# Attention, capped routing, experts and a gated block on one core: conversion in 512 columns, a rewritten compaction, and changed ends of the attention

## The chip, the cores and the metric

The kernel runs on one core of a Trainium2 chip. The metric is the device time of that core in microseconds (us); smaller is better. Five engines run side by side, each with its own queue that it works through in order: PE (matmul), DVE (vector), ACT (scalar), POOL (GpSimd) and SP, which here only issues DMAs. An instruction that waits holds everything behind it in its queue.

## The reference

```
scores = scale * matmul(q_c, [mem_k, k_ctx].T)        # chunk 32, left 16, right 8, 8 memory keys
a = exp(scores - max); a = a / (sum(a) + 1e-9); out_c = matmul(a, [mem_v, v_ctx])
x = out as [3072 tokens, 512]
logits = x @ w_gate                                   # 8 experts
for idx in argsort(-logits.flatten()):                # greedy; 384 tokens for each expert
    token, e = idx // 8, idx % 8
    if token not assigned and count[e] < 384: assign
x[mask_e] = relu(x[mask_e] @ w1[e]) @ w2[e]           # 512 -> 1024 -> 512
h = x @ w_in                                          # 512 -> 1024
solu = h * softmax(h)
ln = (solu - mean) / sqrt(var + 1e-6) * g_ln
return ln @ w_out                                     # 1024 -> 512
```

Everything is float32 at the inputs except `w_in` and `w_out`, which come as float64 (64-bit words) and have to be converted on the chip.

## The kernel before, in words

**Attention** takes 24 tiles of 128 tokens (`NT`). For tile `i` the loop emits parts of five tiles: the sums of tile i-1, the scores of tile i (`s`, PE), their maximum `mx` and the subtraction `p` (DVE), the exponential (ACT, `p<-p`), then the product with `v`, the transposes `xtp`, and the gate's matmuls. SP loads `qt`, `kd` and `vd` of each tile; `kd` and `vd` are rings of 5 and 4 buffers, of which only parts are loaded, so all nine are set to zero at the start. The gate works on four tiles at a time (`gate`, 32 columns of PE for each tile), except in the last four tiles, which `gate_last` takes one by one. Then all logits stand in `L`.

**Routing** goes through 8 rounds; one expert is filled in each. A round takes the maximum `m` of `L`, runs two searches of four steps (`ge` on DVE, `r<-oh,ge` on PE, `sat` on DVE, `second` on PE, `base` on DVE), and then `compact` makes the list `idx` of the 384 tokens of the expert. With it POOL gathers the rows `xg` from DRAM, and `iw` picks the expert's weights.

**Experts** then run on PE, all matmuls as sums of three products of a high and a low part (`xh`, `xl`, `w1h`, `w1l` and so on): `g12` (`h<-xh,w1h` to `y<-hh,w2h`), `g3` (`h<-in_h,yh`) and `g4` (`o<-out_h,lh`). The order is g12(0), g3(0), g12(1), g3(1), g4(0), g12(2), and so on. In the order of emission the routing of round r+1 lies beside round r.

**Conversion** (class `Fixed`) makes `in_h`, `in_l`, `out_h`, `out_l` from the 64-bit `w_in` and `w_out`, in chunks of 256 columns, 16 for each matrix: a DMA `raw`, ACT `v<-raw`, DVE `e<-raw`, `v<-v,e`, `e<-v`, `e<-raw,e`, then ACT `in_h` or `out_h`, and POOL `v<-v,in_h` and `in_l<-v,e` (for `w_out`: POOL `v<-v,e`, ACT `out_h`, DVE or POOL `out_l`). `raw`, `v` and `e` are rings of three.

**What sets the order.** A planner (`Pace`) keeps a modelled clock for each engine. "Beside" jobs (conversion, routing) are generators; when the main stream calls `tick()`, it lets those go on whose next step fits by the model (`limit` bounds the rank of jobs that may run, `late` and `DUE_OUT` push the conversion of `w_out`). The result is a fixed order for each engine; the chip waits only for semaphores. Nearly every instruction is recorded by one helper, line 398 before and 420 after, so rows are told apart by tile names.

Of the kernel before, what the change touches and what calls it, by code (L numbers as in the profile page):

```python
# [48 lines left out]
DUE_OUT = 5.42  # L49
# [11 lines left out]
def attention(nc, tc, q, kx, vx, wgx, ident, x_dram, L, consts, beside):  # L61

    with ExitStack() as ctx:
# [34 lines left out]
        consts()  # L98

# [79 lines left out]
        def gate(u, js=range(4)):  # L179
            if js[0] == 0:  # L180
                G[u] = ps.tile([128, 128], F32, tag="t", name="g")
# [16 lines left out]
        def gate_t(u):  # L198
            g = ps.tile([128, 4, 32], F32, tag="t", name="g")
            nc.tensor.transpose(g, G.pop(u), ident)  # L200
            nc.vector.tensor_scalar(L[:, 4 * u:4 * u + 4, :], g[:, :, 0:E], 0.0, None, op0=ALU.add)

        for i in range(NT + 5):
            n = 0
# [26 lines left out]
            if i > NT:  # L231
                gate_last(i - 5)
# [5 lines left out]
class Pace:  # L238
# [61 lines left out]
    def cost(self, eng, op, outs, ins, kw):  # L300
# [9 lines left out]
        t = (0.108 if op == "transpose" else 0.06 * n / 128 if kw.get("tile_position") else  # L310
# [99 lines left out]
class Fixed:  # L410
# [6 lines left out]
    CHUNK = 256  # L417
# [24 lines left out]
    def chunk(self, m, n, lead=0.0):  # L442
# [6 lines left out]
        if wide:  # L449
            yield from self.take("raw", 3)  # L450
            while self.hold:
                yield 0.0
            r = self.tmp.tile([128, C, 2], I32, tag="raw", name="raw", bufs=3)
# [4 lines left out]
            yield from self.take("v", 3)  # L458
            v = self.tmp.tile([128, C], F32, tag="v", name="v", bufs=3)
            e = self.tmp.tile([128, C], F32, tag="e", name="e", bufs=3)  # L460
            vi, ei, top = v.bitcast(I32), e.bitcast(I32), r[:, :, 1]
            nc.scalar.activation(v, top.bitcast(F32), AF.Copy, scale=2.0 ** -112)
            yield "spare", "dve"
            V.tensor_scalar(ei, top, -0x80000000, None, op0=ALU.bitwise_and)
            yield "act"
# [7 lines left out]
        else:  # L473
            yield from self.take("v", 3)
            v = self.tmp.tile([128, C], F32, tag="v", name="v", bufs=3)
# [44 lines left out]
class Route:  # L520
# [6 lines left out]
    def __init__(self, ctx, nc, tc, L, beside):  # L527
# [4 lines left out]
        self.held, self.stage = False, 0  # L532

    def consts(self):
# [9 lines left out]
        self.tri = k.tile([128, 128], F16, name="tri")  # L544
        V.tensor_scalar(self.tri, self.row, col, None, op0=ALU.is_gt)
# [18 lines left out]
        iota(self.cp[:, :, 0], [[1, NT]], 0, 0)
        V.tensor_copy(self.cp[:, :, 1], col.to_broadcast([128, NT]))
# [99 lines left out]
    def rounds(self):  # L665
# [3 lines left out]
        for r in range(E):  # L669
# [6 lines left out]
            if r + 1 < E:  # L676
# [12 lines left out]
                yield from self.search(lo, oh, zero, r, r + .5)  # L689
                th = self.found  # L690
# [71 lines left out]
    def compact(self, r, s1, sl):  # L762

        nc = self.nc
        V, T = nc.vector, nc.tensor
        low = self.t("low", [NT], I32)
        V.tensor_scalar(low, sl, 127, None, op0=ALU.bitwise_and)
        b = self.t("b", [NT, TT])
        V.tensor_scalar(b[:, :, 2], sl, 256.0, None, op0=ALU.is_ge)
        V.tensor_scalar(b[:, :, 0], sl, 128.0, None, op0=ALU.is_lt)  # L770
        yield "spare", "dve"
        cc = self.t("cc", [2 * TT])
        rhs = self.t("rhs", [NT, 2, TT], BF)
        half, part = NT // 2, NT // 4
        for c0 in (0, half):
            ohl = []
            for c1 in (c0, c0 + part):
                o = self.w.tile([128, part, 128], BF, tag="ohl", name="ohl", bufs=2)
                V.tensor_tensor(o, self.row[:, None, :].to_broadcast([128, part, 128]),
                                low[:, c1:c1 + part, None].to_broadcast([128, part, 128]), op=ALU.is_equal)  # L780
                ohl.append(o)
                if c1 == 0:
                    V.scalar_tensor_tensor(b[:, :, 1], b[:, :, 0], -1.0, b[:, :, 2], op0=ALU.mult, op1=ALU.subtract)
                    V.tensor_scalar(b[:, :, 1], b[:, :, 1], 1.0, None, op0=ALU.add)
                    V.tensor_tensor(b, b, s1[:, :, None].to_broadcast([128, NT, TT]), op=ALU.mult)
                    for a in range(2):
                        V.tensor_tensor(rhs[:, :, a], b, self.cp[:, :, a:a + 1].to_broadcast([128, NT, TT]),
                                        op=ALU.mult)
                yield 0.0
            yield "dve"  # L790
            p = yield from self.take()
            for c in range(half):
                T.matmul(p[:, 0:2 * TT], ohl[c // part][:, c % part],
                         rhs[:, c0 + c].rearrange("p a t -> p (a t)"), start=c == 0, stop=c == half - 1)
            yield "pe"
            if c0 == 0:
                V.tensor_copy(cc, p[:, 0:2 * TT])
            else:
                V.tensor_tensor(cc, cc, p[:, 0:2 * TT], op=ALU.add)
            self.held = False  # L800
        idx = self.k.tile([128, TT], I32, name=f"idx{r}")
        V.scalar_tensor_tensor(idx, cc[:, 0:TT], 128.0, cc[:, TT:2 * TT], op0=ALU.mult, op1=ALU.add)
# [3 lines left out]
class Experts:  # L806
# [159 lines left out]
    def g3(self, r, t, between):  # L966
# [3 lines left out]
        for half in range(2):  # L970
            n = 0
            s = slice(half * 512, half * 512 + 512)
            for dt in range(4):
                self.need("y", r, dt)
                self.fixed.need(0, self.beside, {4 * dt + 2 * half, 4 * dt + 2 * half + 1})
# [273 lines left out]
```

## Time and profile before

| | before |
|---|---|
| median of 3 runs | 793.64 us (793.4 to 796.08) |
| the profiled execution | 792.05 us, span 790.3 us |
| mean granted clock | 0.953 |
| busy PE / DVE / ACT / POOL | 717.0 / 550.4 / 340.9 / 207.4 us |
| chain that ended last | PE 69%, DVE 19%, issue 4%, POOL 3%, ACT 2%, DMA 2% |

In the forty slices of the page PE is at 9 tenths nearly throughout, except in the first six slices (attention, 7 to 9), in slices 7 and 8 (3 and 6; the first routing round) and in slice 15 (4). In that one slice outside the first 160 us PE's clock falls as well. The chain that ended last runs on DVE to about 140 us and on PE after it.

### The profile page before, as it was taken

How to read it: one execution, taken by the hardware profiler on the slowest of the kernel's cores; microseconds unless marked ns; L12 is line 12 of the kernel's file. 1: busy time of each engine (PE TensorE's matmuls, PEld its weight loads, DVE VectorE, ACT ScalarE, POOL GpSimd, SP SyncE). 2: the span in 40 equal slices, each digit the busy share in tenths (PEclk: the TensorE clock that was granted, in tenths of full speed). 3: DMA queues.
4: the chain of work that ended last, by engine and by line, in shares of the span. 5: the costliest groups of instructions: out<-in, count | busy, mean ns of one | idle time of the engine just before them, and what ended most of it. 6: DMA issues, size and time to landing. Idle time of an engine off the chain costs nothing.

```text
span 790.3 us, 14784 instructions
## 1 busy us (share of the span) xinstructions
PE 717.0 (91%) x5728; PEld 619.6 (78%) x5728; DVE 550.4 (70%) x1536; ACT 340.9 (43%) x680; POOL 207.4 (26%) x288
## 2 busy tenths in 40 slices
PE   6988963699999949999999999999999999999993
PEld 5766653688789737998899889888988898899883
DVE  7787967699999974993798389838973952563150
ACT  1566630243574443431653174227324642463170
POOL 4344520631621342003300520052014211400121
PEclk7999995699999978999999999999999999999997
DMA  7999891720620340102600340053006110600100
GB/s 248 336 331 337 292 349 56 231 85 29 219 87 27 100 141 30 64 1 81 213 0 1 128 165 1 1 177 118 1 14 210 70 41 27 209 19 0 41 15 27
DMA packets 32326, 89.37 MB, mean 113 GB/s; under 512 B 4480, under 2 KB 4608, under 8 KB 32256
## 3 DMA queue, kind: packets, MB, share of 16 engines
q0 software_dynamic: 13056, 46.14, 17.2%
q1 hardware_dynamic: 19200, 42.29, 15.6%
q8 instruction: 45, 0.74, 0.4%
q14 instruction: 25, 0.20, 0.1%
HBM read 75.83 MB, written 12.58 MB: 112 GB/s over the span
## 4 chain that ended last, share of the span: by engine, by line
PE 69%; DVE 19%; issue 4%; POOL 3%; ACT 2%; DMA 2%; POOLq 0%; DVEq 0%
PE h L398 30%; PE y L398 17%; PE o L398 15%; DVE e L398 4%; PE tp L398 4%; PE r L398 3%; DVE sum L398 2%; DVE p L398 2%; DVE mx L398 2%; DVE v L398 1%; DMA xg<-x_dram,idx 1%; ACT p L398 1%; DVE ge L398 1%; DVE nm L398 1%; DMA raw<-in_win_dram 1%
## 5 line engine op out<-in xcount | busy, mean ns | idle before, releaser
L398 PE MATMUL y<-hh,w2h 128*128 128x384 f32 x256 | 91.7, 358 | 5.4 <-DVE e L398 5.4
L398 POOL DMA_INDIRECT out_dram<-ob,idx x24 | 26.1, 1089 | 265.6 <-ACT ob L398 223.4
L398 PE MATMUL y<-hl,w2h 128*128 128x384 f32 x256 | 88.9, 347 | 0.1
L398 PE MATMUL o<-out_h,lh 128*128 128x512 f32 x192 | 78.4, 409 | 11.2 <-ACT out_h L398 11.2
L398 PE MATMUL y<-hh,w2l 128*128 128x384 f32 x256 | 87.4, 341 | 0.0
L398 POOL DMA_INDIRECT raw<-in_w_dram,iw x64 | 62.6, 978 | 73.4 <-DVE w1l L398 27.9
L398 PE MATMUL o<-out_l,lh 128*128 128x512 f32 x192 | 76.6, 399 | 1.2 <-DVE out_l L398 1.2
L398 PE MATMUL h<-in_h,yh 128*128 128x512 f32 x192 | 76.7, 399 | 0.0
L398 PE MATMUL h<-in_l,yh 128*128 128x512 f32 x192 | 76.4, 398 | 0.0
L398 PE MATMUL o<-out_h,ll 128*128 128x512 f32 x192 | 76.4, 398 | 0.0
L398 DVE TENSOR_REDUCE nm<-h 128x1 f32<-128x512 f32 x48 | 33.0, 688 | 61.9 <-PE h L398 61.5
L398 PE MATMUL h<-in_h,yl 128*128 128x512 f32 x192 | 75.8, 395 | 0.0
L398 ACT ACTIVATE hh<-h 128x384 fp32r<-128x384 f32 x64 | 31.4, 490 | 81.0 <-PE h L398 71.2
L398 PE MATMUL h<-xh,w1h 128*128 128x384 f32 x256 | 58.3, 344 | 0.7 <-ACT xh L398 0.7
L398 ACT CAST w2h<-raw 128x512 fp32r<-128x512 f32 x64 | 39.5, 619 | 44.8 <-PE y L398 44.8
L398 PE MATMUL h<-xh,w1l 128*128 128x384 f32 x256 | 58.7, 346 | 0.0
L398 PE MATMUL h<-xl,w1h 128*128 128x384 f32 x256 | 56.9, 343 | 0.0
L398 PEld LDWEIGHTS y<-hh,w2h 128*128 128x128 f32 x256 | 48.2, 188 | 7.2 <-DVE e L398 6.8
L398 DVE TENSOR_TENSOR xl<-tp,xh 128x512 fp32r<-128x512 f32 x24 | 16.6, 691 | 50.0 <-ACT xh L398 50.0
L398 PEld LDWEIGHTS o<-out_h,lh 128*128 128x128 f32 x192 | 36.7, 191 | 18.5 <-ACT out_h L398 11.9
L398 ACT ACTIVATE ob<-o,k 128x512 f32<-128x512 f32 x24 | 16.5, 688 | 79.5 <-PE o L398 76.8
L398 DVE TENSOR_TENSOR w2l<-raw,w2h 128x512 fp32r<-128x512 f32 x64 | 44.3, 694 | 7.8 <-ACT w2h L398 7.8
(192 smaller groups left out, 1694.1 us busy)
## 6 DMA issues: line engine op xcount, KB each, us to landing
vd<-in_vx_dram SPq DMA_DIRECT2D x48, 256.0 KB, 4.9
kd<-in_kx_dram SPq DMA_DIRECT2D x48, 176.0 KB, 4.8
qt<-in_q_dram SPq DMA_DIRECT2D x24, 256.0 KB, 4.7
x_dram<-xs SPq DMA_DIRECT2D x6, 1024.0 KB, 10.4
raw<-in_win_dram SPq DMA_DIRECT2D x16, 256.0 KB, 5.0
raw<-in_wout_dram SPq DMA_DIRECT2D x16, 256.0 KB, 2.7
raw<-in_w_dram,iw POOLq DMA_INDIRECT x64, 5.5
xg<-x_dram,idx POOLq DMA_INDIRECT x24, 3.7
```

Source lines behind the costliest of these rows:

```text
L398: return fn(*args, **kw)
```

## The change

1. **Conversion in 512 columns.** `CHUNK` 256 to 512; rings of `raw`, `v`, `e` from three to two; 8 chunks for each matrix instead of 16, 7 instead of 14 of `w_in` beside the attention, every second due time doubled. The first DVE step reads ACT's `v`, not `raw`.
2. **Compaction.** The one-hot of the list's place has 32 columns instead of 128, and the twelve rows of 32 places are in the right operand: 24 matmuls on 32 PE columns, four side by side, then 4 with a constant `rep` that bring the parts together.
3. **The start.** The zeros of `kd` and `vd` are shared by DVE (2), ACT (3) and POOL (4) instead of 5 on DVE and 4 on POOL. `consts` (the routing's constants) is a beside job of the attention, where before all of it stood ahead of the first `mx`.
4. **The attention's end.** From tile 22 `pace.limit = 0` holds the conversions. The last group's gate takes tiles 20 to 22 in 32 columns each and one transposition; only tile 23 has the old form. In round 0 `limit` is 2 after the first search.
5. **First weights.** `w1l` of the first two slices is made after the gather of round 0 is issued; `junk` shares the ring of `ob`; the planner's cost of a matmul in 32 columns has a floor of 0.03 us.

```
-EVERY_OUT = 3.5            +EVERY_OUT = 7.0
-CHUNKS_A = 14              +CHUNKS_A = 7
-EVERY_A = 4.4              +EVERY_A = 8.8
-DUE_OUT = 5.42             +DUE_OUT = 10.84
-    CHUNK = 256            +    CHUNK = 512
```
```diff
-        for i in range(AHEAD):
-            (nc.gpsimd if i % 2 else nc.vector).memset(KD[i], 0.0)
-            if i < AHEAD - 1:
-                (nc.vector if i % 2 else nc.gpsimd).memset(VD[i], 0.0)
+        def clear(t):
+            flat = ...
+            nc.scalar.activation(flat, zero.to_broadcast([128, flat.shape[1]]), AF.Copy)
+        nc.vector.memset(KD[0], 0.0)
+        clear(KD[1])
+        nc.gpsimd.memset(KD[2], 0.0)
+        nc.vector.memset(VD[0], 0.0)
+        clear(KD[3])
+        nc.gpsimd.memset(VD[1], 0.0)
+        clear(VD[2])
+        nc.gpsimd.memset(KD[4], 0.0)
+        nc.gpsimd.memset(VD[3], 0.0)
...
-        consts()
-
+        pace.add(consts(), FIRST_C, 0)
...
         for i in range(NT + 5):
+            if i == NT - 2:
+                pace.limit = 0
...
-            if i > NT:
-                gate_last(i - 5)
+            if NT < i < NT + 4:
+                gate(NT // 4 - 1, (i - NT - 1,), 2)
+            if i == NT + 4:
+                gate_t(NT // 4 - 1, 3)
+                gate_last(NT - 1)
...
-            yield from self.take("raw", 3)
+            yield from self.take("raw", 2)
...
-            V.tensor_scalar(ei, top, -0x80000000, None, op0=ALU.bitwise_and)
             yield "act"
+            yield "spare", "dve"
+            V.tensor_scalar(ei, vi, -0x80000000, None, op0=ALU.bitwise_and)
...
     def compact(self, r, s1, sl):
+        A, idle = CAP // 32, ("spare", "dve") if r else 0.0
-        V.tensor_scalar(low, sl, 127, None, op0=ALU.bitwise_and)
+        V.tensor_scalar(low, sl, 31, None, op0=ALU.bitwise_and)
+        V.scalar_tensor_tensor(am, sl, 32.0, low, op0=ALU.add, op1=ALU.subtract)
+        V.tensor_tensor(am, am, s1, op=ALU.mult)
+        V.tensor_tensor(rhs[:, :, 1], self.atab..., am..., op=ALU.is_equal)
+        V.tensor_tensor(rhs[:, :, 0], rhs[:, :, 1], self.cnum..., op=ALU.mult)
+        V.tensor_scalar(rhs[:, :, 1], rhs[:, :, 1], self.col, None, op0=ALU.mult)
-                o = self.w.tile([128, part, 128], BF, tag="ohl", name="ohl", bufs=2)
+            o = self.w.tile([128, part, 32], BF, tag="ohl", name="ohl", bufs=2)
...
+            T.matmul(p[32 * j:32 * j + 32, 0:2 * A], ohl[c // part][:, c % part],
+                     rhs[:, c].rearrange("p w a -> p (w a)"), start=c < 4, stop=c >= NT - 4,
+                     tile_position=(0, 32 * j), skip_group_check=True)
...
+            T.matmul(p[32 * j:32 * j + 32, 0:2 * TT], self.rep, cc[:, :, :, j], start=True, stop=True,
...
-        self.split_w(0, 0, (1,))
         self.fixed.hold = True
...
-        self.split_w(0, 1, (1,))
+        for f in range(2):
+            self.split_w(0, f, (1,))
```

At the attention's end DVE's queue before, from the last tile's normalisation on (`xt` is a copy of transposed tokens, `L<-g` takes logits, `e` and `v` are conversion); behind the last row stand `xt`, `L`, `e`, `e`, `L` and then `m<-L`:
```order
L398 TENSOR_TENSOR p<-p,rec 128x512
L398 TENSOR_SCALAR e<-raw 128x256 x3
L398 COPY L<-g 128x8
L398 TENSOR_SCALAR L<-g 128x32
L398 SCALAR_TENSOR_TENSOR v<-v,e 128x256
L398 TENSOR_SCALAR e<-v 128x256
L398 SCALAR_TENSOR_TENSOR v<-v,e 128x256 x2
L398 SCALAR_TENSOR_TENSOR e<-raw,e 128x256
L398 TENSOR_SCALAR e<-v 128x256
L398 SCALAR_TENSOR_TENSOR e<-raw,e 128x256
L398 COPY xt<-xtp 128x512
```
The same place in the changed kernel, to the first steps of the search:
```order
L420 TENSOR_TENSOR p<-p,rec 128x512
L420 TENSOR_SCALAR L<-g 128x32
L420 COPY xt<-xtp 128x512 x2
L420 TENSOR_SCALAR L<-g 128x24
L420 COPY L<-sp 128x8
L420 TENSOR_REDUCE m<-L 128x24
L420 TENSOR_TENSOR oh<-L,m 128x192
L420 TENSOR_SCALAR ki<-m 128x24
L420 TENSOR_TENSOR ki<-ki,m 128x24
L420 COPY flags<-rev 128x8
L420 SCALAR_TENSOR_TENSOR ge<-ki,zero,jtab 128x180 x2
L420 TENSOR_SCALAR e<-v 128x512 x2
```
No conversion stands between the last tile's `rec` and `m`; the steps of two chunks of 512 columns now stand inside the first search (the last row is their first).

DVE before, from the first list `idx` on (`xl` and `w1l` are low parts that PE reads in g12(0); `gone` to `ge` begin the search of round 1):
```order
L398 SCALAR_TENSOR_TENSOR idx_2510<-cc 128x3
L398 SCALAR_TENSOR_TENSOR v<-v,e 128x256
L398 TENSOR_SCALAR e<-raw 128x256
L398 TENSOR_TENSOR xl<-tp,xh 128x4x128 x3
L398 TENSOR_TENSOR w1l<-raw_2421,w1h 128x512
L398 TENSOR_TENSOR w2l<-raw_2423,w2h 128x512 x2
L398 TENSOR_SCALAR gone<-s_2447 128x24
L398 TENSOR_TENSOR left<-left,es 128x8
L398 TENSOR_SCALAR el<-es 128x8
L398 TENSOR_TENSOR L<-L,gone 128x192
L398 TENSOR_TENSOR L<-L,el 128x192
L398 TENSOR_REDUCE m<-L 128x24
```
DVE in the changed kernel, from `xl` on:
```order
L420 TENSOR_TENSOR xl<-tp,xh 128x4x128 x3
L420 TENSOR_SCALAR gone<-s_2366 128x24
L420 TENSOR_TENSOR left<-left,es 128x8
L420 TENSOR_SCALAR el<-es 128x8
L420 TENSOR_TENSOR L<-L,gone 128x192
L420 TENSOR_TENSOR L<-L,el 128x192
L420 TENSOR_REDUCE m<-L 128x24
L420 TENSOR_TENSOR oh<-L,m 128x192
L420 TENSOR_SCALAR ki<-m 128x24
L420 TENSOR_TENSOR ki<-ki,m 128x24
L420 SCALAR_TENSOR_TENSOR ge<-ki,zero,jtab 128x360
L420 TENSOR_TENSOR w1l<-raw_2344,w1h 128x512 x2
```
Both `w1l` of the first slices, one of which was made two rows ahead of `idx` before, now come behind the ten steps that open the next search.

POOL before, around g4(0), which begins while the first row runs (`xg` are the gathers for g12(2), `na` to `k` the norm of round 1; the `v` and `out_l` of the last three rows belong to the last chunks of `w_out`):
```order
L398 DMA raw_4299<-in_w_dram,iw_4188 128x1024
L398 DMA xg<-x_dram,idx_4370 128x512 x3
L398 TENSOR_TENSOR na<-s 128x3
L398 TENSOR_SCALAR na<-na 128x3
L398 TENSOR_TENSOR nv<-na 128x3
L398 TENSOR_TENSOR nv<-nv,q 128x3
L398 TENSOR_SCALAR nv<-nv 128x3
L398 TENSOR_TENSOR k<-nv,power 128x3
L398 TENSOR_TENSOR v<-v,e 128x256 x3
L398 TENSOR_TENSOR out_l<-v,out_h 128x256
L398 TENSOR_TENSOR v<-v,e 128x256
```
POOL in the changed kernel, at the same place:
```order
L420 TENSOR_TENSOR k<-nv,power 128x3
L420 TENSOR_TENSOR v<-v,e 128x512 x2
L420 DMA raw_4129<-in_w_dram,iw_4031 128x1024
L420 DMA raw_4131<-in_w_dram,iw_4031 128x1024
L420 DMA raw_4133<-in_w_dram,iw_4031 128x1024
L420 DMA raw_4135<-in_w_dram,iw_4031 128x1024
L420 DMA raw_4137<-in_w_dram,iw_4031 128x1024
L420 DMA raw_4139<-in_w_dram,iw_4031 128x1024
L420 DMA xg<-x_dram,idx_4211 128x512 x3
L420 MEMSET spacer 1x1
L420 DMA out_dram<-ob,idx_2417 3072x512
```
The last `v<-v,e` of the conversion (second row) now stand ahead of the six weight loads, and none stands behind the gathers `xg`.

## Rows read from the trace of the kernel before

**Rows 1.** Windows: span, PE, PEld, DVE, ACT, POOL busy (instructions), clock, DMA share, GB/s
```profile
60.00:80.00 20.00, 17.02 (x395) 13.08 (x389) 15.48 (x41) 11.61 (x25) 8.26 (x10) 1.00 0.96 338
157.00:282.00 125.00, 122.03 (x844) 105.05 (x842) 117.31 (x342) 62.76 (x132) 36.40 (x43) 1.00 0.31 103
282.00:304.00 22.00, 10.03 (x38) 7.06 (x39) 11.96 (x35) 8.59 (x18) 9.76 (x17) 0.61 0.17 54
```
**Rows 2.** Timeline of PE, then DVE, at the start: start, duration, names [idle before, releaser]
```profile
6.82 1.08 PE L398 MATMUL s<-kd,qt 128*32 128x128 f32 x32 [0.93 <-DMA qt<-in_q_dram]
9.83 1.80 PE L398 MATMUL s<-kd,qt 128*32 128x128 f32 x32 [1.93 <-DMA qt<-in_q_dram]
...
11.59 0.69 DVE L398 TENSOR_REDUCE mx<-s 128x8 f32<-128x512 f32 x1
...
14.75 0.64 DVE L398 TENSOR_REDUCE mx<-s 128x8 f32<-128x512 f32 x1
```
**Rows 3.** Waits of DVE, 12 to 104 us: total, times, longest
```profile
DVE sum L398 <- ACT p L398: 8.7, 13, 0.7
DVE e L398 <- DMA raw<-in_win_dram: 2.8, 1, 2.8
```
**Rows 4.** Timeline of DVE, the last tiles of the attention and its end
```profile
93.78 0.64 DVE L398 TENSOR_REDUCE mx<-s 128x8 f32<-128x512 f32 x1
...
100.77 0.69 DVE L398 TENSOR_REDUCE mx<-s 128x8 f32<-128x512 f32 x1
...
104.12 0.69 DVE L398 TENSOR_TENSOR p<-p,rec 128x512 f32<-128x512 f32 x1
...
109.31 0.41 DVE L398 SCALAR_TENSOR_TENSOR v<-v,e 128x256 int32<-128x256 int32 x1
...
112.66 0.68 DVE L398 COPY xt<-xtp 128x512 f32<-128x512 f32 x1
...
116.20 0.35 DVE L398 TENSOR_REDUCE m<-L 128x24 f32<-128x192 f32 x1
```
**Rows 5.** Timeline of DVE, the first round's search and compaction
```profile
121.04 0.15 DVE L398 TENSOR_SCALAR_CACHE_REDUCE sat<-r 15x8 f16<-15x8 f32 x1 [0.21 <-PE r L398]
...
133.24 0.28 DVE L398 TENSOR_SCALAR e<-raw 128x256 int32<-128x256 int32 x1
...
137.88 0.18 DVE L398 TENSOR_SCALAR low<-sl 128x24 int32<-128x24 int32 x1
...
141.52 2.67 DVE L398 TENSOR_TENSOR ohl<-row,low 128x768 bf16<-128x768 bf16 x2
...
145.44 0.16 DVE L398 SCALAR_TENSOR_TENSOR idx<-cc 128x3 int32<-128x3 f32 x1
```
**Rows 6.** Timeline of PE, the search's matmuls and the first of g12(0)
```profile
120.24 0.77 PE L398 MATMUL r<-oh,ge 128*15 128x8 bf16 x24 [0.75 <-DVE ge L398]
...
154.66 1.48 PE L398 MATMUL h<-xh,w1l 128*128 128x384 f32 x4
```
**Rows 7.** Timeline of DVE beside them
```profile
153.87 0.68 DVE L398 TENSOR_TENSOR w1l<-raw,w1h 128x512 fp32r<-128x512 f32 x1
...
157.88 0.59 DVE L398 SCALAR_TENSOR_TENSOR ge<-ki,zero,jtab 128x360 bf16<-128x360 uint16 x1
```
**Rows 8.** Timeline of PE, g4(0) from its first product to g12(2)
```profile
277.36 0.40 PE L398 MATMUL o<-out_h,lh 128*128 128x512 f32 x1
...
293.32 0.80 PE L398 MATMUL o<-out_h,lh 128*128 128x512 f32 x1 [9.60 <-ACT out_h L398]
...
312.99 0.40 PE L398 MATMUL o<-out_h,ll 128*128 128x512 f32 x1
313.22 0.69 PE L398 MATMUL h<-xh,w1h 128*128 128x384 f32 x3
```
**Rows 9.** Timeline of POOL at the same place
```profile
285.02 0.96 POOL L398 DMA_INDIRECT xg<-x_dram,idx  x1 [6.75 <-DVE L L398]
...
291.07 2.13 POOL L398 TENSOR_TENSOR v<-v,e 128x256 f32<-128x256 f32 x3
```

More of the change, by code (lines that the diff above doesn't have):

```diff
@@ L689, in rounds @@
                 yield from self.search(lo, oh, zero, r, r + .5)
+                if not r:
+                    self.beside.limit = 2
                 th = self.found
@@ new lines, in compact @@
+        yield idle
+        V.tensor_scalar(rhs[:, :, 1], rhs[:, :, 1], self.col, None, op0=ALU.mult)
+        ohl, part = [], NT // 2
+        for c in (0, part):
+            yield idle
+            o = self.w.tile([128, part, 32], BF, tag="ohl", name="ohl", bufs=2)
+            V.tensor_tensor(o, self.row[:, None, 0:32].to_broadcast([128, part, 32]),
+                            low[:, c:c + part, None].to_broadcast([128, part, 32]), op=ALU.is_equal)
+            ohl.append(o)
+        if r:
+            yield "dve"
@@ new lines, in compact @@
+        p = yield from self.take()
+        for c in range(NT):
+            j = c % 4
+            T.matmul(p[32 * j:32 * j + 32, 0:2 * A], ohl[c // part][:, c % part],
+                     rhs[:, c].rearrange("p w a -> p (w a)"), start=c < 4, stop=c >= NT - 4,
+                     tile_position=(0, 32 * j), skip_group_check=True)
+        yield "pe"
+        cc = self.t("cc", [2, TT, 4], BF)
+        V.tensor_copy(cc.rearrange("p w t j -> p (w t j)"), p[:, 0:2 * A])
+        self.held = False
@@ L801, in compact @@
+        yield "dve"
+        p = yield from self.take()
+        for j in range(4):
+            T.matmul(p[32 * j:32 * j + 32, 0:2 * TT], self.rep, cc[:, :, :, j], start=True, stop=True,
+                     tile_position=(0, 32 * j), skip_group_check=True)
+        yield "pe"
+        tok = self.t("tok", [TT])
+        V.tensor_scalar(tok, p[:, 0:TT], 128.0, None, op0=ALU.mult)
         idx = self.k.tile([128, TT], I32, name=f"idx{r}")
-        V.scalar_tensor_tensor(idx, cc[:, 0:TT], 128.0, cc[:, TT:2 * TT], op0=ALU.mult, op1=ALU.add)
+        V.tensor_tensor(idx, tok, p[:, TT:2 * TT], op=ALU.add)
@@ L803, in compact @@
+        self.held = False
         self.idx[r] = idx
@@ L1114, in run @@
         self.beside.limit, self.beside.fit = 9, FIT_OUT
-        self.beside.add(self.fixed.all(1, self.beside, EVERY_OUT, 0, 16))
+        self.beside.add(self.fixed.all(1, self.beside, EVERY_OUT, 0, 8))
         start = self.beside.now
-        self.beside.late = lambda: 16 - len(self.fixed.left[1]) < (self.beside.now - start - DUE_FROM) / DUE_OUT - 1
+        self.beside.late = lambda: 8 - len(self.fixed.left[1]) < (self.beside.now - start - DUE_FROM) / DUE_OUT - 0.5
         more = [(0, 0), (0, 1)]
@@ L1191, in step @@
         beside.tick()
-    attention(nc, tc, q, kx, vx, wg, ident, x_dram, L, route.consts, step)
+    attention(nc, tc, q, kx, vx, wg, ident, x_dram, L, lambda: route.consts(ident), beside, step)
+    while route.making:
+        beside.tick()
+    beside.limit = 9
     route.open_psum(ctx)
```

128 lines of the change are left out of this document (62 added, 66 removed).

## The prediction

> **What bounds the kernel now.** I read three views in this order: busy time by windows, then DVE's waits and its timeline in the attention, then the timelines of PE and POOL where PE stops.
>
> The windows give three stages [rows 1]. In the attention, 60 to 80 us for instance, the DMA engines are busy 0.96 of the time at 338 GB/s, while no engine is full (PE 17.02, DVE 15.48 of 20 us). From 157 to 282 us PE is busy 122.03 of 125 us at clock 1.00. From 282 to 304 it is busy 10.03 of 22 us, at clock 0.61: the only place behind the first routing round where PE stands still.
>
> In the attention DVE decides. From 12 to 104 us it waited 8.7 us for ACT's exponential (0.7 each, between `p` and `sum`), and once, 2.8 us, for a conversion's `raw` [rows 3]; for scores or for a tile's loads it never waited. Two `mx` in a row lie 3.16 us apart at the start [rows 2], and 6.99 us between the last two tiles, where conversions stand between them [rows 4]. From there to the first list the chain runs through DVE and PE in turn. So what comes off DVE's queue up to `idx` comes off the time, unless the loads then decide.
>
> At 283 us PE waits 9.60 us for ACT's `out_h` [rows 8]. ACT is not the cause: `out_h` needs POOL's `v<-v,e`, which starts at 291.07, and POOL stood 6.75 us before 285.02 for the routing's `L`, without which the next gather's list is not ready [rows 9]. The `v<-v,e` stood behind those gathers in POOL's queue. It is an order, not a load.
>
> **The change part by part.** The sum is made against the profiled execution, 792.05 us, which is 1.59 under the median of 793.64.
>
> *Start.* Tile 0's scores end at 7.90 us, but its `mx` starts at 11.59 [rows 2], behind DVE's five zeros and all constants. In the new order DVE has two zeros and no constants; at the rate of `mx` (512 columns in 0.69 us) their 3456 columns take 4.7 us at most, from about 1 us on, so they are done before the scores. Tile 1's scores, which wait for `qt` and end at 11.63, then limit: the second `mx` comes at 11.65 instead of 14.75, **-3.1**. ACT's three zeros are not in the trace. At the same rate their 4864 columns end near 8 us, at one and a half times that near 11, and the first exponential would be due near 9.4; so 0 to +2. The constants go into the 0.7 us for which DVE waits on ACT in each tile; if they don't fit, part of the 3.69 us between 7.90 and 11.59 comes back.
>
> *Conversion beside the attention.* A DVE step on 256 columns takes 0.41 us, or 0.28 for the simple ones [rows 4, 5], so a chunk 1.4 and two of them 2.8. At 512 columns the four steps take 0.69, 0.69 (as `p` and `mx`, 512 columns) and twice some 0.5: 2.2 to 2.4. Six such chunks in the chain instead of ten of 256 columns are 13 to 14 us either way. What changes is the end: with the conversions held from tile 22, the last 6.99 us gap [rows 4] becomes 3.2 or 3.9, **-3.5** (-3.1 to -3.8). The wait of 2.8 for `raw` could go too, or come back twice as long with twice the bytes: I take 0, with -2.8 to +5.6. Against the gain stands the DMA at 0.96: a faster DVE asks for the loads sooner.
>
> *Tail.* Between 109.31 and 112.66 DVE did little but conversions, while the transposed tokens waited for their copy `xt` [rows 4]: 3.35 us, which now stand nowhere in the order. Another 0.7 lay between the last `L`; the gate of three tiles in one pass replaces three single ones, and gives a PSUM buffer back. I take **-3.5** of the 12.1 us from `rec` of the last tile to `m`; bounds -2 and -5.
>
> *First search.* A step without conversions is [rows 5] 0.21 us of wait before `sat` and 0.28 before `base`; a conversion step that is put there costs its length less that wait. The two held chunks put seven steps of 0.5 to 0.7 us into such places: 0.45 (two beside the first step, whose wait is longer), then about 0.41, 0.34, 0.41, 0.48, 0.27 and 0.48: 2.84. Before, the search and the steps behind it held some 0.8 of such work, which goes. POOL works on these chunks at the same time, and both slow each other: `ohl` x2 took 2.67 us, 1.33 each [rows 5], where 768 columns at the rate of `mx` would be 1.03. I add 0.7: **+2.7** (+2 to +6).
>
> *Compaction.* `low` to the end of `idx` takes 7.72 us [rows 5]. New: `low` and `am` 0.6, three passes over 288 columns some 1.3, two one-hots of 384 columns 0.5 each, 24 matmuls as in the search (0.77, [rows 6]) of which half lie beside the second one-hot, `cc`, 4 matmuls, `tok` and `idx` with four changes of engine at 0.2 to 0.3: 4.9. **-2.8** (-2 to -3.5).
>
> *First weights.* PE's first `w1l` product starts at 154.66, right behind DVE's `w1l` of 153.87 [rows 6, 7]. Now the ten steps that end with `ge` (157.88 + 0.59) come ahead of it. Without the `w2l` between, they take 2.8 us; `w1l` is that much later, and PE's queue stands on it with everything behind: **+2.7**. It is less if the search's matmuls, which stand behind the first such product, would have cost PE 0.6 later (+2), and more if PE's clock rises later after the pause (+4).
>
> *The stall.* From the first product of g4(0) to g12(2) it is 35.86 us [rows 8]. The work in it is 72 products at 0.23 us, the distance of the last ones at full clock [rows 8], 16.5 us, twelve transposes of 128 columns (0.7 to 1.4, one to two products for each four) and the compaction's matmuls (0.8, [rows 6]): 18.5. In the new order the last `v<-v,e` stand ahead of the weight loads, before g4(0), so nothing of `w_out` waits for the next list: -17.3. Next in line are the gathers for g12(2): three issues of about 1 us [rows 9] and a landing lie between `idx` and their transposes, for which PE has products to do; I leave +0.5: **-16.8** (-14 to -17.3). The conversion that stood in the pause has to be done in the 125 us before, where DVE has 7.7 us left [rows 1]. Four old chunks are 4 x 1.9 = 7.6; the merged steps and the two cheaper compactions give back about 10. So it fits, but its cover is thin.
>
> *Compaction on PE, rounds 1 to 7.* 28 short matmuls instead of 24, about 0.2 us more for each round, PE being the bound: **+1.2**. DVE's relief is beside PE.
>
> Sum: -3.1 - 3.5 - 3.5 + 2.7 - 2.8 + 2.7 - 16.8 + 1.2 = **-23.1**: 768.9 for a profiled run, 770.5 as a median.
>
> **The rivals.** *A. The loads decide in the attention.* For it: 0.96 and 338 GB/s [rows 1]. Against it: DVE never waited for a tile's loads, only for ACT and once for `raw` [rows 3]. Then start and last gap give nothing, 770.5 + 6.6 = **777**. The Trainium skill ("DMA: Bandwidth & Descriptors", section "Specifications") gives a core about 358 GB/s from HBM, and the 338 of the row lie close under it, so the trace agrees that little room is left. The 100.77 us to the last `mx` hold at most 34 MB at the row's rate; at the page's they would take an estimated 95 us, about where the forecast puts the last `mx`.
>
> *B. The stall moves.* The conversion of `w_out` is only shifted; if DVE or POOL run late in the 125 us by the thin cover above, PE meets the same wait earlier, in front of another product. Half of it staying (8.5 us, and the low clock of 0.61 with it) gives **779**; all of it, 787. For it: DVE at 117.31 of 125 us. Against it: the compaction and the merged steps take more off DVE than is put on.
>
> *C. DVE and POOL lock each other out.* If a POOL addition holds DVE for its whole length, the two held chunks cost the search more: four POOL steps of up to 1.4 us (twice 2.13 / 3, [rows 9]) are 5.6, of which DVE would lose some 4 instead of 0.7: **774**. The row of `ohl` shows 1.33 against 1.03, a slowing and not a standstill. The Trainium skill ("SBUF — State Buffer", section "Who interferes with whom") says that VectorE and GpSimd share a port pair under an exclusive lock and that one fully blocks; it speaks against conversions in the search, and the trace bears it out in part only.
>
> *D. Slower.* `raw` is twice as large and its ring has two buffers, so each chunk's load starts only when DVE is done with the chunk but one before, and the load shares a DMA that is 0.96 busy. If each of the remaining five chunks makes DVE wait as the one before did, twice as long (5.6 us, [rows 3]), with everything of the attention queued behind it in order, that is 28 us: **798**. It decides from 4.6 us a chunk on. Against it: nine of ten such loads made no wait before.
>
> **How the numbers follow.** Forecast 0.58; A 0.14; B 0.13; C 0.10; D 0.05. The bounds of the terms, taken together, move the forecast by some 6 us, so 764 to 778 is its own range. With A and C inside, and half of B, the range is 761 to 783; what is left out is D, most of B's worse half and a gain beyond the terms. Half a per cent, about 4 us, is what a measurement can tell from no change. Faster by more, under 789.7: 0.93. Within: 0.03 (D at less than its price, or A and all of B together). Slower: 0.04 (D).
>
> **What would show it.** Right: second `mx` near 11.7 us; last `mx` near 94 and `m<-L` near 106; `low` to `idx` under 5 us; a wait of PE of 2 to 3 us for DVE's `w1l`; g4(0) to g12(2) under 20 us with the clock at 1.00; rounds of the same length behind that, about 76 us. Wrong: `e<-v` or `v` waiting for `raw` several times (D); `mx` waiting for PE's `s`, and that for `qt` or `kd` (A); a new wait of PE for `out_h`, `in_h` or `hl` in g12(0) to g3(1) (B); steps of the search over 3 us (C).

## The result, and the profile after

The changed kernel takes 786.03 us (median of four runs, 784.96 to 789.37) against 794.86 us (793.4 to 797.55): ratio 0.9897, 95% interval 0.9868 to 0.9927. It is faster, by 8.8 us where 23 were forecast, and outside the range of 761 to 783. The profiled span is 784.3 us, 6.0 less than before.

The table sets points of the two timelines beside each other: the second tile's `mx`, the last `mx`, the first `m<-L`, `low`, the end of the first `idx`, the first `w1l` product, the first products of g3(0) and g4(0), and the first of g12(2).

| stretch | before, us | after, us | difference | forecast |
|---|---|---|---|---|
| start to second `mx` | 14.75 | 11.64 | -3.1 | -3.1 |
| to the last `mx` | 86.02 | 88.50 | +2.5 | -3.5 |
| to `m<-L` | 15.43 | 14.14 | -1.3 | -3.5 |
| to `low` (search) | 21.68 | 25.31 | +3.6 | +2.7 |
| to the end of `idx` (compaction) | 7.72 | 5.20 | -2.5 | -2.8 |
| to the first `w1l` product | 9.06 | 11.95 | +2.9 | +2.7 |
| to g3(0) | 44.72 | 48.95 | +4.2 | 0 |
| to g4(0) | 77.98 | 81.84 | +3.9 | 0 |
| g4(0) to g12(2) | 35.86 | 18.75 | -17.1 | -16.8 |
| to the end | 477.08 | 478.02 | +0.9 | +1.2 |

The windows of the changed kernel that answer to [rows 1]:
```profile
60.00:80.00 20.00, 16.83 (x388) 13.04 (x388) 17.40 (x34) 11.18 (x22) 10.20 (x9) 1.00 0.99 352
...
157.00:282.00 125.00, 118.57 (x803) 103.47 (x804) 111.29 (x286) 55.77 (x107) 34.61 (x33) 0.95 0.24 79
282.00:304.00 22.00, 22.00 (x127) 17.35 (x126) 13.94 (x46) 15.23 (x29) 11.49 (x19) 1.00 0.60 202
```
The stall is gone: PE is busy in all of 282 to 304 us. But in the 125 us before it PE now works 118.57 instead of 122.03 us, at clock 0.95 instead of 1.00. In the attention the DMA share rose from 0.96 to 0.99.

DVE's timeline of the changed kernel, at the places of [rows 2], [rows 4] and [rows 5]:
```profile
8.48 0.69 DVE L420 TENSOR_REDUCE mx<-s 128x8 f32<-128x512 f32 x1
11.64 0.64 DVE L420 TENSOR_REDUCE mx<-s 128x8 f32<-128x512 f32 x1
...
100.14 0.69 DVE L420 TENSOR_REDUCE mx<-s 128x8 f32<-128x512 f32 x1
...
114.28 0.35 DVE L420 TENSOR_REDUCE m<-L 128x24 f32<-128x192 f32 x1
...
119.88 2.50 DVE L420 SCALAR_TENSOR_TENSOR ge<-ki,base,jtab 128x180 bf16<-128x180 uint16 x2
...
123.93 1.73 DVE L420 SCALAR_TENSOR_TENSOR ge<-ki,base,jtab 128x180 bf16<-128x180 uint16 x2
...
139.59 0.18 DVE L420 TENSOR_SCALAR low<-sl 128x24 int32<-128x24 int32 x1
...
144.63 0.16 DVE L420 TENSOR_TENSOR idx<-tok,r 128x3 int32<-128x3 f32 x1
```
POOL's timeline beside the search:
```profile
119.13 1.70 POOL L420 TENSOR_TENSOR v<-v,in_h 128x512 f32<-128x512 f32 x1 [20.22 <-DVE sat L420]
120.91 1.26 POOL L420 TENSOR_TENSOR in_l<-v,e 128x512 fp32r<-128x512 f32 x1
124.04 1.42 POOL L420 TENSOR_TENSOR v<-v,in_h 128x512 f32<-128x512 f32 x1 [1.86 <-ACT in_h L420]
```
The second `mx` came at 11.64 us as forecast, 3.1 earlier, and the last one at 100.14, only 0.6 earlier. The two `ge` that lie beside POOL's additions took 2.50 and 1.73 us for a pair that otherwise takes 0.72.

What PE waited for in the changed kernel, 157 to 287 us (total, times, longest), the three largest:
```profile
PE y L420 <- DVE e L420: 2.9, 2, 1.8
PE r L420 <- DVE ge L420: 2.7, 5, 0.8
PE h L420 <- DVE w1l L420: 2.5, 1, 2.5
```
In the same stages before (155 to 277 us) its three waits for DVE were 0.8, 0.6 and 0.6 us.

PE in these stages, from the first `w1l` product to g4(0), before and then in the changed kernel:
```profile
154.66:277.36 122.70, 120.15 (x824) 104.36 (x824) 115.01 (x338) 60.80 (x129) 37.36 (x44) 0.99 0.29 96
156.74:287.53 130.79, 124.36 (x826) 108.16 (x827) 116.76 (x306) 59.71 (x115) 38.92 (x37) 0.95 0.27 88
```
The stretch is 8.1 us longer with the same products. Of that, 3.9 are idle time of PE (2.55 before, 6.43 after), and 4.2 are products that took longer while the granted clock was lower (0.95 instead of 0.99).

### The profile page after: what moved, and what is told of

Its sections match the earlier page's. It is cut to its first block, busy times and chain, and to the rows that moved or that the text cites. A ratio compares the mean times of both kernels' runs of the same rounds, so it can differ in the third digit from the quotient of the medians.

```text
span 784.3 us, 14637 instructions
## 1 busy us (share of the span) xinstructions
PE 714.1 (91%) x5761; PEld 615.3 (78%) x5761; DVE 525.1 (67%) x1430; ACT 341.0 (43%) x650; POOL 198.9 (25%) x263
## 4 chain that ended last, share of the span: by engine, by line
PE 71%; DVE 17%; DMA 3%; ACT 3%; issue 3%; POOL 1%; SPq 0%; POOLq 0%; DVEq 0%; ACTq 0%
PE h L420 32%; PE y L420 16%; PE o L420 14%; PE tp L420 4%; DVE e L420 3%; PE r L420 3%; DVE sum L420 2%; DVE ge L420 2%; DVE p L420 2%; DVE mx L420 1%; DMA xg<-x_dram,idx 1%; DMA qt<-in_q_dram 1%; ACT p L420 1%; DVE v L420 1%; DVE w1l L420 1%
## 5 line engine op out<-in xcount | busy, mean ns | idle before, releaser
L420 PE MATMUL y<-hl,w2h 128*128 128x384 f32 x256 | 88.5, 346 | 0.0
L420 POOL DMA_INDIRECT out_dram<-ob,idx x24 | 24.3, 1012 | 227.5 <-ACT ob L420 227.1
L420 PE MATMUL h<-xl,w1h 128*128 128x384 f32 x256 | 58.5, 348 | 0.0
L420 PEld LDWEIGHTS h<-xh,w1l 128*128 128x128 f32 x256 | 46.4, 194 | 3.3 <-DVE w1l L420 3.2
L420 ACT ACTIVATE e<-h,nm 128x512 f32<-128x512 f32 x48 | 32.5, 683 | 37.5 <-issue 23.1
```

The lines of the kernel that those rows point to most:

```text
L420: return fn(*args, **kw)
```

## The experiments

Each is a single run beside 794.7 to 795.3 us of before on the same chip, except `c6_best`, a median of four. Four runs of the changed kernel spread over 4.4 us, so single times that differ by less are not told apart, and lengths of stages are compared instead.

**What holds the attention.** `s1_zeros_alone` gives before the shared zeros alone:
```diff
-            (nc.gpsimd if i % 2 else nc.vector).memset(KD[i], 0.0)
+        nc.vector.memset(KD[0], 0.0); clear(KD[1]); nc.gpsimd.memset(KD[2], 0.0) ...
```


> Before, with the zeros of kd and vd shared by DVE, ACT and POOL as in the changed kernel and nothing else. Theory, the loads decide: second mx at 11.6 us, but last mx at 99.5 to 101 as before, time 793 to 796. Rival, DVE's chain decides: last mx at 97 to 98, time 790 to 792.

793.95 us. Its DVE timeline:
```profile
12.95 0.64 DVE L410 TENSOR_REDUCE mx<-s 128x8 f32<-128x512 f32 x1
...
101.95 0.69 DVE L410 TENSOR_REDUCE mx<-s 128x8 f32<-128x512 f32 x1
```
The second `mx` is 1.8 us earlier than before (11.6 was expected), the last one 1.2 later. The loads take the earlier start: PE waits 2.2 us for `vd` at 43 us, and a conversion's `raw` lands when it landed before. The rows of that wait, before and then in s1:
```profile
74.48 0.29 DVE L398 TENSOR_SCALAR e<-raw 128x256 int32<-128x256 int32 x1 [2.76 <-DMA raw<-in_win_dram]
74.36 0.29 DVE L410 TENSOR_SCALAR e<-raw 128x256 int32<-128x256 int32 x1 [3.27 <-DMA raw<-in_win_dram]
```
Behind it s1 loses 1.2 us more at a granted clock of 0.57 from 76 to 84 us, where before had 1.00; so the last `mx` tells less than the `raw` does.

`a1_loads_only` and `a2_no_loads` take the changed kernel and leave out the work on `w_in`, the second its loads too:
```diff
             nc.scalar.activation(v, top.bitcast(F32), AF.Copy, scale=2.0 ** -112)
+            if m == 0:                       # a1
+                nc.scalar.copy(hi, v); nc.scalar.copy(lo, v)
+                ... return
+        if m == 0:                           # a2, ahead of the load
+            nc.scalar.activation(hi, self.g[:, 0:1].to_broadcast([128, C]), AF.Copy)
+            ... return
```


> The changed kernel, but each chunk of w_in is only loaded and copied: raw as before, ACT's v, and in_h and in_l are plain copies of v by ACT; DVE's four steps and POOL's two additions on w_in are left out, so the output is not the reference's. It tells what held the attention at 512 columns (last mx 100.14 us; 94.52 with 256). Theory, POOL's long additions and DVE's steps: last mx 91 to 94, m to low 20.8 to 21.2. Rival, the loads of 512 KB between those of kd and vd: last mx 98 to 101.

> The changed kernel without any conversion of w_in and without its loads: in_h and in_l are filled by ACT from a constant, so the output is not the reference's. It tells whether the bytes of w_in hold the attention. Theory, the loads decide: with loads but no steps the last mx came at 98.27 us and PE waited 10.4 us for vd; without the loads' 3.5 to 4 MB, 10 to 12 us at 338 GB/s, it comes at 86 to 90, PE's waits for vd under 3 us. Rival, the chain of DVE, ACT and PE: 94 or later.

The last `mx` on DVE's timeline, of a1 and then of a2:
```profile
98.27 0.69 DVE L420 TENSOR_REDUCE mx<-s 128x8 f32<-128x512 f32 x1
```
```profile
90.99 0.69 DVE L420 TENSOR_REDUCE mx<-s 128x8 f32<-128x512 f32 x1
```
PE's wait for `vd` from 8 to 100 us (total, times, longest), of a1 and then of a2:
```profile
PE o L420 <- DMA vd<-in_vx_dram: 10.4, 9, 2.9
```
```profile
PE o L420 <- DMA vd<-in_vx_dram: 2.6, 4, 1.2
```
With the loads and none of the conversion's steps on DVE and POOL the last `mx` is at 98.27 (779.27 us in all); without the loads at 90.99 (768.84 us), one microsecond above the 86 to 90 expected. The same attention with everything stood at 100.12 to 101.98 in seven kernels. So my first expectation for a1 was the wrong one, and its rival held. But a1 isn't the changed kernel less some steps: its third and fourth `raw` are asked for at 48.46 and 56.38 us instead of 54.01 and 64.94, and in the changed kernel PE waited for `vd` only 3.1 us, not 10.4. The 7 us between a1 and a2 are therefore not what the loads cost the changed kernel.

`a3_no_pool` keeps DVE's steps and leaves out only POOL's additions on `w_in`:
```diff
-            yield "spare", "pool"
-            G.tensor_tensor(v if wide else lo, v, hi.bitcast(F32), op=ALU.subtract)
-            if wide:
-                G.tensor_tensor(lo, v, e, op=ALU.add)
+            nc.scalar.copy(lo, e)
```


> The changed kernel with DVE's steps on w_in kept and only POOL's two additions of each chunk left out (in_l is a copy of e by ACT, so the output is not the reference's). Theory, that POOL's additions of 512 columns hold DVE: no DVE step of a few columns takes over 0.6 us in the attention, last mx 94 to 96, and ge x2 beside the held chunks is back at 0.72, m to low 22.5 to 23.5. Rival, DVE's own longer steps: last mx 98 to 100, m to low near 25.

777.75 us; last `mx` at 96.22, `m` to `low` 21.82 instead of 25.31. Its `ge` at the same two steps of the search:
```profile
113.69 0.72 DVE L420 SCALAR_TENSOR_TENSOR ge<-ki,base,jtab 128x180 bf16<-128x180 uint16 x2
115.96 0.72 DVE L420 SCALAR_TENSOR_TENSOR ge<-ki,base,jtab 128x180 bf16<-128x180 uint16 x2
```
Without POOL's additions DVE's pairs are at 0.72 again: the hold is theirs. In the attention it is the same. Two conversion steps on DVE in the changed kernel, beside two additions (61.49 to 64.17 us), and the same two in a3:
```profile
61.58 1.47 DVE L420 TENSOR_SCALAR e<-v 128x512 int32<-128x512 int32 x1
63.08 1.64 DVE L420 SCALAR_TENSOR_TENSOR v<-v,e 128x512 int32<-128x512 int32 x1
```
```profile
65.61 0.42 DVE L420 TENSOR_SCALAR e<-v 128x512 int32<-128x512 int32 x1
66.06 0.69 DVE L420 SCALAR_TENSOR_TENSOR v<-v,e 128x512 int32<-128x512 int32 x1
```
That a3 ends its attention 2 us before a1, which does less, follows from the loads in a1: PE waits 3.0 us for `vd` in a3, as in the changed kernel.

DVE works through its queue in order, so the rows of its timeline from the second to the last `mx` add up to that stretch (sums of rows, in us):

| what DVE's time went to | before | changed | a3 | a1 |
|---|---|---|---|---|
| `mx`, `p`, `sum<-p`, `rec`, gate | 52.8 | 52.7 | 52.9 | 53.8 |
| `sum<-sum`, 22 steps of eight columns | 4.4 | 7.3 | 4.5 | 4.4 |
| conversion | 17.2 | 13.3 | 12.4 | 0 |
| the routing's constants | 0 | 2.8 | 2.7 | 2.9 |
| wait for ACT's exponential | 7.4 | 10.0 | 10.0 | 13.2 |
| wait for PE's scores | 0 | 1.8 | 1.1 | 9.0 |
| wait for `raw` | 2.8 | 0 | 0 | 0 |
| wait for the gate and for POOL's `p` | 1.5 | 0.6 | 0.3 | 3.6 |
| second to last `mx` | 86.0 | 88.5 | 83.9 | 86.8 |

So three things ate what the changed kernel saved on the conversion and on `raw`: the hold by POOL (2.9 us on steps of eight columns alone), the constants, which did not vanish in the waits for ACT, and one wait for scores, behind a late `vd`. The last two, in the changed kernel:
```profile
32.41 1.03 PE L420 MATMUL o<-vd,pt 128*32 128x128 f32 x26 [0.82 <-DMA vd<-in_vx_dram]
...
36.43 0.69 DVE L420 TENSOR_REDUCE mx<-s 128x8 f32<-128x512 f32 x1 [1.75 <-PE s L420]
...
40.13 0.95 DVE L420 TENSOR_TENSOR up<-own,off 128x64 f32<-128x64 f16 x1
```
DVE's queue still decides this attention: a3 takes 4.6 us off that stretch with the loads at the same share of the DMA (0.98 instead of 0.96). The loads are what comes next, as a1's 9.0 us show.

**512 columns, alone and undone.**
```diff
-    CHUNK = 256                              # u1: before with part 1 alone
+    CHUNK = 512
-    CHUNK = 512                              # u2: the changed kernel without part 1
+    CHUNK = 256
```


> Before, with the conversion in 512 columns alone (ring of two, doubled spacing and due times; junk in the ring of ob and four scratch tiles shared, to make room); zeros, constants, compaction, tail and first weights are those of before. Theory: the stall at 283 us goes by this part alone, since no conversion of w_out stands behind the gathers in POOL's order any more: g4(0) to g12(2) 18 to 19 us instead of 35.86, and the time near 778 to 782 (794 less 17, and 1 to 5 back because POOL's additions on 512 columns hold DVE longer). Rival: the 512 columns also bring the 8 us that the changed kernel loses between g12(0) and g4(0), by a fuller DVE: then 784 to 788.

> The changed kernel with the conversion back in 256 columns (ring of three, old spacing and due times), all other parts kept. Theory: the stall is back (g4(0) to g12(2) 34 to 37 us), because conversions of w_out stand behind the gathers in POOL's order again; the stage from g12(0) to g4(0) is short again by 4 us or more; time 792 to 798. Rival: the other parts (start, tail, compaction) carry most of the gain by themselves: 784 to 788.

u1: 784.97 us, g4(0) to g12(2) 18.22. u2: 792.53 us, 35.33. So the stall goes with the 512 columns, and these alone give as much as the whole change, within what single runs tell. But in u1 the stretch from the first `w1l` product to g4(0) is 134.8 us instead of 122.7, and that is the rival's price: 12 of the 17.6 us come back there.

u2's last `mx` is at 94.52, where I had forecast it; but its order has only seven chunks of 256 columns finished by then, that of before ten and the changed kernel five of 512, which are the same columns as ten. It moved work and loads, it didn't save them.

**The search, the first weights, the end.** Three single edits to the changed kernel:
```diff
-    beside.limit = 9                         # u3, behind the attention
+    beside.limit = 2
+        self.split_w(0, 0, (1,))             # u4, ahead of the compaction
-            if NT < i < NT + 4:              # u5
-                gate(NT // 4 - 1, (i - NT - 1,), 2)
+            if i > NT:
+                gate_last(i - 5)
```


> The changed kernel with the two held chunks of w_in kept out of the first round's search as well (the limit is 2 behind the attention instead of 9); they are converted later. Theory, that POOL's additions of 1.3 to 1.7 us hold DVE's search steps (ge x2 took 2.50 and 1.73 us instead of 0.72): m to low falls from 25.31 us to 20.8 to 21.2, and the time by 3 to 4.5, to 781 to 783. Rival: the chunks are missed by g3(0) or fill DVE in g12(0), which gives it back: 785 to 788.

> The changed kernel with the first w1l made in the compaction again, and both w1l ahead of the next search's first steps, as before. Theory: PE's wait of 2.45 us for w1l goes, and with it the half clock up to 162 us: from idx to g3(0) 56 to 58 us instead of 61.06, time 781 to 783. Rival: PE then waits as long for the search's ge and sat that came earlier: 785 to 787.

> The changed kernel with the last four tiles' logits by four single passes as before (in the spare PSUM buffer). Theory, that PE's own order is the bound of the end: from the last mx to m 13.6 to 14.2 us either way (14.14 to 14.15 in the changed kernel), since only conversions ahead of m made it 15.43 before. Rival, the gate of three tiles in one pass carries the gain: 15 or more.

u3: 788.81 us. `m` to `low` falls to 21.05, 4.3 us less, as expected; but to g3(0) it is 52.64 instead of 48.95, and g4(0) to g12(2) 23.06 instead of 18.75. The two chunks cost at least as much where they went, and the time lies beyond the rival's 785 to 788.

u4: 783.48 us. From `idx` to the first `w1l` product 8.90 us instead of 11.95, 3 us less: later `w1l` was a plain loss. Behind it the changed kernel runs at the lower of the clock's two levels:
```profile
156.00:162.00 6.00, 5.26 (x37) 4.45 (x38) 4.15 (x11) 1.00 (x2) 2.40 (x2) 0.50 0.36 114
```
u4 has 0.98 there, but 0.60 from 162 to 166. To g3(0) it takes 48.05 instead of 48.95; u5, with the same order as the changed kernel there, took 50.02, so these 0.9 us are not told from scatter.

u5: 786.97 us. From the last `mx` to `m` 13.45 us, 0.7 less than with the gate of three tiles. The changed kernel's PE at the end, where its queue has hardly a gap from 103.31 on, and then a single pass of u5:
```profile
106.50 0.66 PE L420 MATMUL xtp<-ident,xs 128*128 128x128 f32 x4
107.09 1.06 PE L420 MATMUL sp<-xt,wg 128*32 128x128 f32 x8
108.08 0.33 PE L420 MATMUL g<-ident,gs 128*128 128x128 f32 x1
108.33 1.08 PE L420 MATMUL o<-vd,pt 128*32 128x128 f32 x32
109.35 0.66 PE L420 MATMUL xtp<-ident,xs 128*128 128x128 f32 x4
109.93 1.06 PE L420 MATMUL sp<-xt,wg 128*32 128x128 f32 x8
```
```profile
111.03 0.96 PE L417 MATMUL sp<-wg,xt 128*128 128x8 f32 x8
```
With the conversions gone from DVE, PE's own order sets the end, and there the new gate takes 1.06 us for a tile where a single pass takes 0.96. What the part gained, 1.3 us, came from fewer conversion steps ahead of `m`. That the hold was needed for it isn't shown: u1, with 512 columns, the old gate and no hold, took 13.64.

**The stage from g12(0) to g4(0).** `o1_out_no_pool` leaves out POOL's additions on `w_out`; b1, c2, c3 and c6 make them on DVE; c1 leaves them on POOL. Where `w_in` is in 256 columns, 14 chunks have the old spacing beside the attention:
```diff
-                yield "spare", "pool"        # o1
-                G.tensor_tensor(v, v, e, op=ALU.add)
-                G.tensor_tensor(v, v, e, op=ALU.add)      # b1, c2, c3, c6
+                V.tensor_tensor(v, v, e, op=ALU.add)
...
-            if n % POOL_OUT == 0:            # o1, b1, c2, c3, c6: all out_l on DVE
+            if False:
...
-    CHUNK = 512                              # c1, c2: w_in, w_out
+    CHUNK = 256, 512
+        while (0, 1, 1) not in self.WS:      # c1, c2, c3
+            tick()
```


> The changed kernel with POOL's additions on w_out left out (v<-v,e is skipped and out_l is made by DVE alone, so the output is not the reference's). It tells what costs the 8 us between g12(0) and g4(0) (48.95 against 44.72, and 46.14 against 41.06 us). Theory, POOL's additions hold DVE there too: the two come back by 5 us or more, time 778 to 781. Rival, DVE's queue is simply full and in another order: 2 us or less, 782 to 785.

> The changed kernel with w_in in 256 columns again (ring of two) and w_out in 512, the first two w1l forced ahead of the next search, and the planner's RUSH raised to 1.2 so that no conversion of w_out stands behind the gathers before g4(0). Theory: the attention of the 256 columns (last mx 94 to 95), the short start of g12(0) (idx to first w1l product 9 us) and no stall (18 to 20 us): 771 to 776. Rival: the w_out conversions that are pushed into g3(0) and g12(1) fill DVE and cost PE what the attention gives: 779 to 784.

> Before, with one edit: the addition v<-v,e of each chunk of w_out and all out_l are made by DVE, so that POOL has no part in w_out's conversion; 256 columns, everything else as before. Theory: the stall of 36 us is an order of POOL's queue, so it goes or shrinks to under 25 us, while DVE takes 16 additions of 0.41 us more but is no longer held by POOL's: 778 to 784. Rival: DVE is full between g12(0) and g4(0), and PE loses there what the stall gives back: 788 to 794.

> The changed kernel with w_in in 256 columns (ring of two), w_out in 512 with its additions on DVE, and the first two w1l ahead of the next search. Theory: the attention of 256 columns (last mx 94 to 96), idx to first w1l 9 us, no stall (18 to 20 us), g12(1) without POOL's hold (40 to 43 us): 768 to 774. Rival: the conversions are planned late here, and DVE's end of them is waited for in g4(0) (stall 25 us or more): 779 to 786.

> The changed kernel (512 columns for both) with w_out's additions on DVE and the first two w1l ahead of the next search. Theory, that POOL's hold costs more than the additions themselves (8 x 0.69 us on DVE): g12(0) and g12(1) together 88 to 91 us instead of 95.1, idx to first w1l 9 us, stall gone: 774 to 778. Rival: DVE is the bound in this stage whoever holds it: 780 to 784.

> The changed kernel with w_out's additions on DVE and the first w1l made as early as before (as in u4; in c3 they were forced behind xl). Theory: idx to first w1l 9 us, g12(1) 42 to 44 us, stall gone, 778 to 782, that is 0.978 to 0.985 of before. Rival: no better than u4 (783.5), since DVE is full either way.

o1: 778.73 us. From the first `w1l` product to g4(0) 121.76 us instead of 130.79, less than before's 122.70; PE is idle there for 1.5 us instead of 6.4, at a clock of 0.97:
```profile
158.37:280.13 121.76, 120.29 (x826) 105.34 (x827) 110.61 (x308) 58.44 (x113) 25.24 (x27) 0.97 0.28 94
```
In the changed kernel DVE's `nm` of one column beside two additions, and POOL's rows there:
```profile
219.96 2.05 DVE L420 TENSOR_TENSOR nm<-nm 128x1 f32<-128x1 f32 x1
```
```profile
219.42 1.32 POOL L420 TENSOR_TENSOR out_l<-v,out_h 128x512 fp32r<-128x512 f32 x1
220.66 1.31 POOL L420 TENSOR_TENSOR v<-v,e 128x512 f32<-128x512 f32 x1
```
The same `nm` in o1:
```profile
220.39 0.16 DVE L420 TENSOR_TENSOR nm<-nm 128x1 f32<-128x1 f32 x1
```
An addition of 512 columns thus takes up to 1.3 us off DVE. Later PE waits for DVE's `e` (here a step of the block's softmax, not of the conversion), and its clock falls behind the wait; that this very wait goes back to the additions is argued from o1, where it is gone. PE's waits in the changed kernel, and the windows over them:
```profile
233.22 0.44 PE L420 MATMUL y<-hh,w2h 128*128 128x384 f32 x1 [1.82 <-DVE e L420]
...
235.12 0.69 PE L420 MATMUL y<-hh,w2h 128*128 128x384 f32 x1 [1.10 <-DVE e L420]
```
```profile
226.00:236.00 10.00, 6.24 (x33) 4.83 (x32) 9.60 (x28) 6.14 (x13) 2.58 (x5) 0.92 0.33 105
236.00:246.00 10.00, 10.00 (x51) 9.62 (x50) 4.99 (x13) 5.22 (x10) 0.92 (x2) 0.74 0.00 0
```
b1: 794.9 us; g4(0) to g12(2) 31.83. Its order at the attention's end came out another, too (19.01 us from the last `mx` to `m`, 15.43 before), so its time says little. With POOL out of `w_out`'s conversion altogether, PE still waits for `out_h`:
```profile
294.08 0.80 PE L398 MATMUL o<-out_h,lh 128*128 128x512 f32 x1 [5.35 <-ACT out_h L398]
...
300.59 0.79 PE L398 MATMUL o<-out_h,lh 128*128 128x512 f32 x1 [3.52 <-ACT out_h L398]
```
So POOL's order was how the stall showed, not why it was there: the last chunks weren't converted by then. DVE's steps on them stand from 286.85 to 300 us in b1.

c1: 795.04 us, c2: 797.75 us, both beyond their rivals too. They have the short attention of 256 columns (95.83 and 95.32, with six chunks finished instead of ten) and the early `w1l`, and lose it all: g4(0) to g12(2) is 33.24 and 39.26 (PE waits there 7.6 us for DVE's `ohl` in c1, 9.4 for ACT's `out_h` in c2), and g3(0) waits 3.2 and 5.0 us for POOL's `in_l`, since fewer chunks are done early. c3: 781.89 us; g12(0) and g12(1) 91.4 instead of 95.1 (slightly over the 88 to 91 expected), g3(0) 2.9 more. c6: 783.10 us (782.03 to 783.68), 0.9849 of before (0.9821 to 0.9877), the same as u4 within the scatter. Its g12(0) and g12(1) take 88.0 us, but its g3(0) takes 6.4 more, 5.5 of it a wait of PE for ACT's `xh`; why that comes late stays open. The additions on DVE gain nothing over POOL's hold: that rival was right. c6's gain over the changed kernel, 2.9 us, is about that of the early `w1l` (8.81 us from `idx`).

## Why the prediction was wrong

- **Start, -3.1.** Right at the second `mx`, and lost by the last. The step that failed is "The constants go into the 0.7 us for which DVE waits on ACT in each tile": they took 2.8 us of DVE, half of them at other places (the row of `up`, 40.13), and DVE's waits for ACT grew by 2.7 instead of shrinking. 1.8 more went to a wait for scores behind `vd`. That is rival A's sign, once; A, with 0.14, has this much of its 6.6 us. "DVE decides" held, but "what comes off DVE's queue" was not added up: the constants were put back into that queue. The rate that the Trainium skill states ("DMA: Bandwidth & Descriptors", section "Specifications"), about 358 GB/s, is not quite a ceiling here: the changed kernel's windows from 20 to 100 us have 318 to 352 GB/s, but o1 has 360 from 60 to 80, and a3 364 from 80 to 96 us.
- **Conversion beside the attention, -3.5.** DVE's conversion steps did shrink, by 4.0 us, and its wait of 2.8 for `raw` went. The step that failed is that POOL's additions cost DVE nothing beside the attention, a term put at nothing without a reason (the prediction charged them in the search alone): they cost 2.9 on the steps of `sum`, and a3 without them ends the attention 3.9 earlier. The last gap is 5.1 us (95.03 to 100.14), not 3.2 to 3.9, 0.9 of it on such a step. Start and this term together: -0.6 instead of -6.6.
- **Tail, -3.5.** -1.3. I took out what stood on DVE and didn't add up PE's queue behind it, which is as long (u5).
- **First search, +2.7.** +3.6, within the bounds given, by luck: two sizes were wrong and nearly cancel. POOL's hold was put at 0.7 and took 3.2 by its rows (2.50, 1.73 and 0.62 us for steps of 0.72, 0.72 and 0.23; a3, which also has two conversion steps fewer there, is 3.5 shorter). DVE's own steps were put at 2.84 and cost some 1.1 over u3's 21.05. Rival C was right in mechanism: the Trainium skill's exclusive lock ("SBUF — State Buffer", section "Who interferes with whom") agrees with `nm` at 2.05 and `ge` at 2.50 us, and only the row of `ohl` [rows 5] was too weak a test of it.
- **Compaction, -2.8, and first weights, +2.7.** -2.5 and +2.9: right. Not counted behind the late `w1l` was the clock of 0.50 up to 162 us; what it cost isn't told from scatter.
- **The stall, -16.8.** -17.1: right at its place. The step that failed is its cover, "so it fits, but its cover is thin". It didn't fit: g12(0) to g4(0) became 8.1 us longer, 3.9 by waits of PE and 4.2 by the lower clock. Busy time said that DVE had 7.7 us left, and DVE's busy time hardly grew (115.0 to 116.8); it didn't say that POOL's additions make DVE stand, or that PE's clock falls behind such waits (0.74 in the row above). In size this is rival B, "half of it staying (8.5 us)", but not by its sign: PE waited for DVE's `ge` and `e`, never for `out_h`, `in_h` or `hl`. The cause is C's, which the prediction priced in the search alone; o1 takes 9.0 us off this stretch. I had the rivals one by one and no sum of two: 768.9 + 6.0 (start and conversion) + 8.1 + 2.2 (tail) + 0.9 (search) is 786.1, the profiled 786.17.
- **Rounds 1 to 7, +1.2.** +0.9: right.

## What to carry to other kernels

When one stall goes because work is done earlier, charge that work to the stage where it lands, with what it does to its neighbours there, not with busy time alone. Where one engine's queue decides, add up that queue before and after, with what was moved into it and with what holds it; a forecast of gaps alone misses both. Where a long instruction on one engine holds another, its length counts on both; moving it across gained nothing here (c6 783.10, u4 783.48 us).

## What the runs showed of the hardware

A DVE instruction on a single column took 2.05 us beside two POOL additions of 512 columns, 0.16 without them; a pair of `ge` 2.50 against 0.72. POOL's own additions took 1.26 to 1.70 us in that company. In the attention, too, DVE's step on `sum`, of eight columns, took 1.06 us at 97.89 where it takes 0.17 elsewhere; two conversion steps took 1.47 and 1.64 us instead of 0.42 and 0.69. In the changed kernel the granted clock was 0.50 from 236 to 240 us, behind waits of PE of 1.82 and 1.10 us, and 1.00 again from 242 us.
